# Holding back the q, k loads of later batches, and moving an interleave to the end of DVE's work, in a fused attention and MLP kernel

## The chip, the cores and the metric

The kernel runs on one core of a Trainium2 chip. The metric is device time in microseconds (us), the median of several executions; a profile is one execution, recorded by the hardware. Its "span" is a little shorter than the time (356.0 us against 357.73 us for the profiled execution of the kernel before).

Engines: PE multiplies matrices, ACT (ScalarE) does exp and gelu, DVE (VectorE) does copies, masks and reductions, POOL (GpSimd) is here mostly an issuer of DMAs, and SP (SyncE) is only an issuer of DMAs. Both issuers feed the same 16 DMA engines, through two queues: q0 is POOL's, q1 is SP's. (From 66 to 78 us of the profile before, the packets of q0 and q1 take 92.0% and 27.7% of the time of the 16 engines, over 100% together.)

## The reference

Attention with a causal mask and a cumulative decay over 8 batches, 8 heads, 576 positions and 64 channels, whose output, seen as 4608 tokens of 512 channels, goes through a two-layer MLP with an exact gelu.

```python
def _attn_ref(q, k, v, s):                      # (8, 8, 576, 64), s (8, 8, 576)
    scores = scale * np.matmul(q, k.transpose(0, 1, 3, 2))
    cum = np.cumsum(np.maximum(s, 0.0), axis=-1)
    bias = -(cum[:, :, :, None] - cum[:, :, None, :])
    scores = np.where(causal, -1000000000.0, scores + np.minimum(bias, 0.0))
    ...                                         # softmax over the last axis
    return np.matmul(attn, v)

def _moe_ref(x, w_in, w_out):                   # x (4608, 512), 512 -> 2048 -> 512
    h = x @ w_in
    g = 0.5 * h * (1.0 + erf(h * inv_sqrt2))
    return g @ w_out
```

## The kernel before

The MLP works through 9 chunks of 512 tokens, counted from 0. Chunk c does its own two layers and, between the matmuls of its second layer, the attention of batch c + 1 in four head pairs. So each chunk has the same work on PE, up to chunk 6.

Each batch's q and k take this path:

1. POOL loads them from HBM, cast to bf16, into one of **three** buffers (`bufs=3`), four loads to a batch. POOL issues them in program order, each as soon as its buffer is free: batch b + 3 follows when batch b has been consumed.
2. DVE interleaves the two heads of each pair (`interleave`).
3. SP writes the rows to a scratch in HBM (`write_rows`).
4. SP reads them back with DMA transposes into `qkT` (`transpose_rows`). Only then can PE compute scores.

Besides the interleave, DVE scales v, masks the exponentials of the scores before PE multiplies them with v, and takes maxima of q, k and v for a check of their range (`absmax`, `absmax_v`); `cert_decay` is one more such check, of the decay.

v goes another way: SP loads it, in five loads to a batch, with rows of 256 bytes. SP issues everything in program order, so the rows of a batch wait on SP behind the v loads of that batch (batch 2's rows, interleaved by 66.1 us, were issued at 81.75, after v loads whose issue ended at 80.27).

```python
def load_early(b, n, p, both=False):
    src = q if n == "q" else k
    if p == 0:
        early[b, n] = work.tile([128, 2, 2, G * D], bf16, tag=f"raw{n}", bufs=3, name=f"early_{n}")
    e0 = (p // 2) * 64
    out = early[b, n][e0 : e0 + 64, p % 2]
    if both:
        out = early[b, n][e0 : e0 + 64].rearrange("g j e f -> g (j e) f")
    ap = [[G * D, 64], [S * D, 4 if both else 2], [1, G * D]]
    nc.gpsimd.dma_start(out=out, in_=bass.AP(tensor=src.tensor, offset=..., ap=ap))

def load_qk(b):
    for p in (0, 2):
        for n in "qk":
            load_early(b, n, p, both=True)
...
# before the chunks
nc.gpsimd.tensor_copy(pace[:64], raws[1, "v"][:64, ST - 1, 0, 0:1])
load_qk(2)
load_qk(3)

for c in range(NCH):
    nb = c + 1
    ...                                          # first-layer matmuls, part 1
    if 0 < c and nb < B:
        if nb + 1 < B:
            load_v(nb + 1, [nc.sync])
        scale_v(nb, STS, nc.vector)
        if nb + 1 < B:
            for i, n in enumerate("qk"):
                interleave(nb + 1, n)
                write_rows(nb + 1, i, nc.sync)
            if nb + 2 < B:
                load_qk(nb + 2)
        absmax_v(nb)
    if c == 0:
        absmax_v(0)
    if c < B:
        for p in range(NP):
            absmax(c, p)
    for f2 in range(3, FT // 2):
        l1_item(c, f2)
    if c == 0:
        ...                                      # attention of batch 1; load_v(2); interleave(2),
        absmax_v(1)                              # write_rows(2), transpose_rows(2, p)
        cert_decay()
    elif nb < B:
        exp_set()
        l2_item(c, 0, 0, 4)
        sc_item(nb, 0)                           # scores of pair 0: needs qkT of batch nb
        l2_item(c, 0, 4)
        for p in range(1, NP):
            if nb + 1 < B:
                transpose_rows(nb + 1, p - 1)
            sc_item(nb, p)
            av_item(nb, p - 1)
            ...
```

The `pace` copy is a device that this kernel used already: a 128x1 copy on POOL that reads a tile. POOL works in order, so every load behind it waits until that tile has been written (the profile before has the copy at 51.58 us, after 21.33 us of waiting for v of batch 1, and batch 2's first load at 52.03). (`qkT`, as well as the v tile of a batch, has two buffers.)

Of the kernel before, what the change touches and what calls it, by code (L numbers as in the profile page):

```python
# [19 lines left out]
def kernel(  # L20
# [10 lines left out]
    nc = tc.nc  # L31
# [7 lines left out]
    B, H, S, D = q.shape  # L39
# [4 lines left out]
    NP = H // 2  # L44
# [51 lines left out]
# [9 lines that stand above are left out]
        nc.gpsimd.dma_start(  # L105
            out=out,
            in_=bass.AP(tensor=src.tensor, offset=src.offset + (b * H + 2 * p) * S * D, ap=ap),
        )
# [24 lines left out]
    qkT = [const.tile([128, 2, NP, 640], bf16, name=f"qkT{i}") for i in range(2)]  # L133
# [11 lines left out]
# [4 lines that stand above are left out]
# [3 lines left out]
    def interleave(b, n):  # L152
        i = 0 if n == "q" else 1
        t = qk_of[b, i] = work.tile([128, 2, G, 2, D], bf16, tag="qkbf", bufs=2, name="qk_bf")
        for j in range(2):
            nc.vector.tensor_copy(  # L156
                t[:, j].rearrange("g r e d -> g e r d"),
                early[b, n][:, j].rearrange("g e (r d) -> g e r d", r=G),
            )
# [3 lines left out]
    def write_rows(b, i, eng):  # L163
        rows_of[b, i] = t = dram.tile([2, 2, S, 128], bf16, name=f"rows{b}_{i}")
        eng.dma_start(
            out=t.rearrange("j a (g r) c -> (a g) j (r c)", r=G),
            in_=qk_of.pop((b, i)).rearrange("p j r e d -> p j (r e d)"),
        )
# [8 lines left out]
    def load_v(b, engs):  # L177
        if (b, "v") not in raws:
            v_tile(b)
        t = raws[b, "v"]  # L180
        for st in range(ST):
            n_st = 128 if st < ST - 1 else SL
            engs[st % len(engs)].dma_start(  # L183
                out=t[:n_st, st, :, :],
                in_=bass.AP(
                    tensor=v.tensor,
                    offset=v.offset + b * H * S * D + st * 128 * D,
                    ap=[[D, n_st], [S * D, H], [1, D]],
                ),
            )  # L190

    def absmax(b, p):

        nc.vector.tensor_reduce(  # L194
            amx[:, b * NP + p], qkT[b % 2][:, :, p, :S], axis=AX, op=ALU.max, apply_absolute_value=True
        )
# [238 lines left out]
    def av_rest(b, p):  # L435
        if p == 0:
            rest_of[b] = ps.tile([128, 2, NP, SL], fp32, tag="av", bufs=3, name="avr")
        for den in range(2):
            av_mm(b, p, rest_of[b][:, den, p], [(jt, 0, n, off) for jt, n, off in REST], den)

    def norm_rest(b):
        t = rest_of[b].rearrange("d n p i -> d n (p i)")
        norm(b, 0, NP, t[:, 0], t[:, 1], CUT, S, [(2, 0, NP * SL)])


    gT_of = {}
# [3 lines left out]
    def l1_item(c, f2, k0=0, k1=None, av=False):  # L450
        k1 = KO if k1 is None else k1
        if c not in gT_of:
            gT_of[c] = work.tile([128, FT, NB], bf16, tag="gT", bufs=1, name="gT")
        if k0 == 0 and av:
            h_of[c, f2] = [ps.tile([128, NB], fp32, tag="av", bufs=3, name="h1_ps") for _ in range(2)]
        elif k0 == 0:
            h_ps = ps.tile([128, 2, NB], fp32, tag="sc", bufs=2, name="h_ps")
            h_of[c, f2] = [h_ps[:, 0], h_ps[:, 1]]
            hh_of[c, f2] = h_ps
        for i in range(2):  # L460
            ft = f2 * 2 + i
            for ko in range(k0, k1):
                nc.tensor.matmul(  # L463
                    h_of[c, f2][i], lhsT=w_in_r[:, ko, ft * 128 : (ft + 1) * 128],
                    rhs=xT[:, ko, c * NB % XW : c * NB % XW + NB],
                    start=(ko == 0), stop=(ko == KO - 1),
                )
        if k1 == KO and f2 < FT // 2 - 1 and not av:
            nc.scalar.activation(gT_of[c][:, f2 * 2 : f2 * 2 + 2, :], hh_of[c, f2], func=AF.Gelu)  # L469
        elif k1 == KO:  # L470
            for i in range(2):
                nc.scalar.activation(gT_of[c][:, f2 * 2 + i, :], h_of[c, f2][i], func=AF.Gelu)  # L472
# [20 lines left out]
    def exp_set():  # L493
        nc.scalar.preload_act_table_set("natural_log_exp_and_others")
# [4 lines left out]
    pace = const.tile([128, 1], fp32, name="pace")  # L499

    def tr_pair(b, p):
        tr_item(b, p, 0)
        tr_item(b, p, 1)
# [47 lines left out]
    for c in range(NCH):  # L551
        nb = c + 1
        l1_item(c, 0, 0, KO - 1)
        l1_item(c, 1, 0, KO - 1)
        if c == 0:
            for p in range(NP):
                av_rest(0, p)
            norm_rest(0)
        l1_item(c, 0, KO - 1)
        l1_item(c, 1, KO - 1)  # L560
        l1_item(c, 2, av=True)
        if 0 < c and nb < B:
            if nb + 1 < B:
                load_v(nb + 1, [nc.sync])
            scale_v(nb, STS, nc.vector)
            if nb + 1 < B:
                for i, n in enumerate("qk"):
                    interleave(nb + 1, n)
                    write_rows(nb + 1, i, nc.sync)
                if nb + 2 < B:  # L570
                    load_qk(nb + 2)
            absmax_v(nb)
        if c == 0:
            absmax_v(0)
        if c < B:
            for p in range(NP):
                absmax(c, p)
        for f2 in range(3, FT // 2):
            l1_item(c, f2)
        if c == 0:  # L580
            exp_set()
            l2_item(c, 0, av=True)
            tr_pair(1, 0)
            tr_pair(1, 1)
            l2_item(c, 1, 0, 4)
            tr_pair(1, 2)
            l2_item(c, 1, 4, 8)
            tr_pair(1, 3)
            sc_item(1, 0)
            l2_item(c, 1, 8)  # L590
            load_v(2, [nc.sync])
            sc_item(1, 1)
            l2_item(c, 2, 0, 6, av=True)
            sc_item(1, 2)
            scale_pair(1, 0)
            l2_item(c, 2, 6, 12, av=True)
            sc_item(1, 3)
            l2_item(c, 2, 12, av=True)
            scale_pair(1, 1)
            l2_item(c, 3, 0, 4)  # L600
            interleave(2, "q")
            write_rows(2, 0, nc.sync)
            av_item(1, 0, rest=False)
            scale_pair(1, 2)
            scale_pair(1, 3)
            l2_item(c, 3, 4, 8)
            interleave(2, "k")
            write_rows(2, 1, nc.sync)
            av_item(1, 1, wide=True, rest=False)
            l2_item(c, 3, 8, 12)  # L610
            for p in (0, 1):
                transpose_rows(2, p)
            av_rest(1, 0)
            av_rest(1, 1)
            av_item(1, 2, wide=True)
            l2_item(c, 3, 12)
            av_item(1, 3)
            norm_rest(1)
            for p in (2, 3):
                transpose_rows(2, p)  # L620
            absmax_v(1)
# [4 lines that stand above are left out]
            sc_item(nb, 0)  # L626
# [6 lines that stand above are left out]
                l2_item(c, p, 0, 12)  # L633
                if p == NP - 1:
                    if nb + 1 < B:
                        transpose_rows(nb + 1, p)
                    av_item(nb, p)
                    norm_rest(nb)
                l2_item(c, p, 12)
        else:  # L640
            if c == B - 1:
                cert_1()
            for sub in range(4):
                l2_item(c, sub, av=sub % 2 == 0)
                if c == B - 1 and sub < 3:
                    (cert_2, cert_3, cert_4)[sub]()
# [151 lines left out]
```

## Time and profile before

| | before |
|---|---|
| time, median of 3 | 357.71 us (356.89 to 358.71) |
| span of the profiled execution | 356.0 us |
| PE busy | 322.6 us |
| mean granted clock of PE (1 is full speed) over the run | 0.972 |

The page of the profile: the span in 40 slices of 8.9 us; each digit is tenths of busy share, or tenths of full clock for PEclk.

```profile
PE   2788999992369999999999999999999999999993
...
PEclk9999999998569999999999999999999999999998
DMA  8999989999999599679346915773440110011011
```

Between its start and its end PE is busy nearly all the time, except in slices 9 to 11 (counted from 0), some 80 to 106 us, where its clock falls too. The DMA engines are at 80% or more nearly all the time up to there. The stage table puts a number on it; its windows run from the first first-layer matmul of one chunk to that of the next, for chunks 1, 2 and 3, and its columns are the length of the window, busy time of each engine with the number of instructions, granted clock, DMA share and GB/s.

```profile
67.44:121.19 53.75, 38.90 (x271) 19.13 (x265) 27.60 (x59) 25.47 (x38) 4.28 (x7) 0.84 1.07 207
121.19:155.75 34.56, 34.56 (x266) 17.66 (x265) 22.25 (x41) 23.95 (x35) 2.45 (x4) 1.00 0.87 188
155.75:190.30 34.55, 34.55 (x265) 17.64 (x264) 22.24 (x40) 23.94 (x35) 0.00 (x0) 1.00 0.61 134
```

Chunk 1 takes 53.75 us for work that takes chunks 2 and 3 34.56 and 34.55 us: 19.2 us are lost there. PE's timeline (start, duration, and in brackets the idle time before it with its releaser):

```profile
94.36 1.03 PE L357 MATMUL sc_ps<-qkT 64*128 64x256 bf16 x10 [12.07 <-DMA qkT<-rows]
95.33 5.14 PE L482 MATMUL o_ps<-w_out_r,gT 128*128 128x512 bf16 x12
103.26 0.76 PE L357 MATMUL sc_ps<-qkT 64*128 64x256 bf16 x10 [2.79 <-DMA qkT<-rows]
```

PE waits 12.07 us for batch 2's first transposes and 2.79 us for the second pair's. Twelve second-layer matmuls right after the long wait take 5.14 us, at a granted clock of 0.53; in other chunks they take 2.76.

The chain of waits, followed back from PE, in order of time (start, duration, what):

```profile
55.49 0.48 SPq L183
...
58.34 7.79 SPq L183
...
66.17 6.86 SPq L183
...
73.07 7.20 SPq L183
...
82.23 7.45 DMA rows<-qk_bf
...
92.21 11.00 DMA qkT<-rows
```

Line 183 is the issue of a v load. SP is stuck in the five v loads of batch 2 from 55.49 to 80.27 us, so it issues the rows of batch 2 at 81.75, although DVE had finished the interleave at 66.1. What POOL issues at that time (its timeline; the first line belongs to batch 4, the second to batch 5, the third to batch 6):

```profile
56.85 0.71 POOL L105 DMA_DIRECT2D early_q<-in_q_dram  x1
...
65.26 1.02 POOL L105 DMA_DIRECT2D early_q<-in_q_dram  x1 [1.45 <-DVE vv L211]
...
89.50 0.61 POOL L105 DMA_DIRECT2D early_q<-in_q_dram  x1 [18.33 <-DVE qk_bf L156]
```

And the DMA queues between 66 and 78 us (packets, MB, share of the time of 16 engines):

```profile
q0 software_dynamic: 1765, 1.91, 92.0%
q1 hardware_dynamic: 1764, 0.44, 27.7%
```

Both queues move the same number of packets, 1765 and 1764, while q0 moves over four times the bytes. (In each stretch of 2 us from 62 to 82 us the two counts differ by at most 2, for instance 295 and 293 from 66 to 68.) From 12 us and 16 engines, one pair takes 12,000 x 16 / 1765 = 109 ns. A 256 KB v load is 1024 rows of 256 bytes. Spread evenly that is 64 to an engine, and 64 x 109 ns = 7.0 us: an estimate, and close to what an issue takes there (6.86 to 7.79 us).

### The profile page before, as it was taken

What the parts mean: (1) busy time and instruction counts of PE and PEld (TensorE: products, weight loads), DVE (VectorE), ACT (ScalarE), POOL (GpSimd) and SP (SyncE); (2) the same over time, 40 slices, a digit from 0 to 9 for tenths busy, and PEclk for the clock granted to TensorE, in tenths of its full rate; (3) what the DMA queues carried; (4) which work ended last, traced back from release to release, by engine and by line L of the source; (5) the groups of instructions that cost most, each with busy time, mean ns of one, the idle gap of its engine ahead of it and who ended that gap; (6) DMA issues with size and microseconds to landing.
All of it is one profiled execution on the core that took longest, in us unless ns stands there. A gap on an engine that the chain in (4) does not pass through costs nothing.

```text
span 356.0 us, 6297 instructions
## 1 busy us (share of the span) xinstructions
PE 322.6 (91%) x2538; PEld 164.6 (46%) x2538; DVE 197.8 (56%) x387; ACT 202.1 (57%) x286; POOL 39.1 (11%) x63
## 2 busy tenths in 40 slices
PE   2788999992369999999999999999999999999993
PEld 1554454640135545544554445445544554444441
DVE  5596476952934595469446934784476448050021
ACT  2776618773233768576867577667676757403500
POOL 6593016300200020000000000000000000000000
PEclk9999999998569999999999999999999999999998
DMA  8999989999999599679346915773440110011011
GB/s 161 156 202 174 197 167 186 199 198 275 126 193 289 149 181 271 137 136 256 46 115 134 225 49 125 150 196 64 125 65 0 47 45 31 0 62 58 1 61 65
DMA packets 88244, 47.30 MB, mean 133 GB/s; under 512 B 68176, under 2 KB 80464, under 8 KB 88208
## 3 DMA queue, kind: packets, MB, share of 16 engines
q1 hardware_dynamic: 75216, 33.19, 40.2%
q0 software_dynamic: 12992, 13.63, 24.0%
q8 instruction: 22, 0.36, 0.4%
q14 instruction: 14, 0.11, 0.1%
HBM read 36.85 MB, written 16.52 MB: 150 GB/s over the span
## 4 chain that ended last, share of the span: by engine, by line
PE 70%; DMA 14%; SPq 9%; POOL 4%; ACT 1%; DVE 1%; issue 0%; ACTq 0%
PE o_ps L482 31%; PE h_ps L463 27%; SPq L183 7%; DMA early_k<-in_k_dram 6%; PE sc_ps L357 4%; PE avn L385 4%; DMA raw_v<-in_v_dram 3%; DMA qkT<-rows 3%; PE avd L385 3%; DMA rows<-qk_bf 2%; POOL P L377 1%; PE avr L385 1%; POOL w_in_r L228 1%; POOL w_out_r L228 1%; POOL P L372 1%; SPq L172 1%
## 5 line engine op out<-in xcount | busy, mean ns | idle before, releaser
L482 PE MATMUL o_ps<-w_out_r,gT 128*128 128x512 bf16 x576 | 136.0, 386 | 0.0
L463 PE MATMUL h_ps<-xT,w_in_r 128*128 128x512 bf16 x576 | 126.3, 379 | 1.3 <-DVE xT L418 0.7
L363 ACT ACTIVATE P<-sc_ps 128x1024 bf16<-128x1024 f32 x64 | 62.0, 1021 | 60.6 <-PE sc_ps L357 60.5
L463 PEld LDWEIGHTS <-w_in_r 128*128 128x128 bf16 x576 | 56.1, 98 | 69.1 <-issue 1.9
L482 PEld LDWEIGHTS <-gT 128*128 128x128 bf16 x576 | 53.6, 99 | 62.9 <-issue 3.8
L469 ACT ACTIVATE gT<-h_ps 128x1024 bf16<-128x1024 f32 x54 | 54.3, 1023 | 47.1 <-PE h_ps L463 47.0
L489 DVE COPY o_sb<-o_ps 128x512 f32<-128x512 f32 x36 | 24.8, 688 | 59.1 <-PE o_ps L482 59.1
L372 DVE TENSOR_TENSOR P<-P,tri_bf 128x512 bf16<-128x512 bf16 x61 | 25.7, 424 | 44.3 <-ACT P L363 43.6
L194 DVE TENSOR_REDUCE amx<-qkT 128x2 f32<-128x1152 bf16 x32 | 40.9, 1333 | 0.0
L357 PE MATMUL sc_ps<-qkT 64*128 64x256 bf16 (+2 forms) x320 | 22.9, 270 | 18.5 <-DMA qkT<-rows 14.9
L418 DVE SCALAR_TENSOR_TENSOR xT<-avn,ln 128x256 bf16<-128x256 f32 (+3 forms) x64 | 21.6, 385 | 26.2 <-ACT ln L403 26.2
L211 DVE TENSOR_TENSOR vv<-raw_v,wb 128x512 bf16<-128x512 f32 (+2 forms) x46 | 27.2, 645 | 9.1 <-DMA raw_v<-in_v_dram 9.1
L357 PEld LDWEIGHTS <-qkT 64*128 64x128 bf16 x320 | 14.2, 100 | 33.7 <-DMA qkT<-rows 16.1
L402 ACT ACTIVATE ln<-avd 128x256 f32<-128x256 f32 x56 | 18.6, 390 | 12.1 <-PE avd L385 12.0
L403 ACT ACTIVATE ln<-ln 128x512 f32<-128x512 f32 (+1 forms) x40 | 23.5, 587 | 1.3
L472 ACT ACTIVATE gT<-h_ps 128x512 bf16<-128x512 f32 x36 | 19.6, 602 | 6.3 <-PE h_ps L463 6.3
L201 DVE TENSOR_REDUCE amv<-raw_v 128x1 f32<-128x2048 f32 (+1 forms) x16 | 22.9, 1468 | 0.0
L385 PEld LDWEIGHTS <-vv 128*64 128x64 bf16 x384 | 17.7, 115 | 8.5 <-issue 4.0
L105 POOL DMA_DIRECT2D early_q<-in_q_dram x18 | 12.0, 664 | 58.2 <-DVE qk_bf L156 52.9
L385 PEld LDWEIGHTS <-wb 128*64 128x64 bf16 x384 | 18.1, 117 | 0.4
L385 PE MATMUL avn<-P,vv 128*64 128x256 bf16 x224 | 17.0, 276 | 0.2 <-DVE vv L211 0.2
L385 PE MATMUL avd<-P,wb 128*64 128x256 bf16 x224 | 16.2, 269 | 0.0
(81 smaller groups left out, 140.1 us busy)
## 6 DMA issues: line engine op xcount, KB each, us to landing
out_dram<-o_sb SPq DMA_DIRECT2D x36, 256.0 KB, 2.2
raw_v<-in_v_dram SPq DMA_DIRECT2D x32, 256.0 KB, 5.3
rows<-qk_bf SPq DMA_DIRECT2D x12, 576.0 KB, 5.0
early_q<-in_q_dram POOLq DMA_DIRECT2D x14, 288.0 KB, 11.5
early_k<-in_k_dram POOLq DMA_DIRECT2D x14, 288.0 KB, 12.7
w_in_r<-in_moe_w_in_dram POOLq DMA_DIRECT2D x4, 512.0 KB, 8.2
w_out_r<-in_moe_w_out_dram POOLq DMA_DIRECT2D x4, 512.0 KB, 10.9
raw_v<-in_v_dram SPq DMA_DIRECT2D x8, 128.0 KB, 5.2
```

The costliest lines, as they stand in the source:

```text
L183: engs[st % len(engs)].dma_start(out=t[:n_st, st, :, :], in_=bass.AP(tensor=v.tensor, offset=v.offset + b * H * S * D + st * 128 * D, ap=[ ...
L194: nc.vector.tensor_reduce(amx[:, b * NP + p], qkT[b % 2][:, :, p, :S], axis=AX, op=ALU.max, apply_absolute_value=True)
L211: eng.tensor_tensor(vb[:n_st, st0:st1, h0:h1, :], t[:n_st, st0:st1, h0:h1, :], wb[:n_st, st0:st1, b * H + h0 : b * H + h1] .unsqueeze(3).t ...
L357: nc.tensor.matmul(s_ps[:, e, off : off + n], lhsT=qkT[b % 2][e * 64 : e * 64 + 64, 1, p, jt * 128 : jt * 128 + 128], rhs=qkT[b % 2][e * 6 ...
L363: nc.scalar.activation(P[:, :, UO[u] : UO[u] + UW[u]], s_ps[:, :, : UW[u]], func=AF.Exp, scale=scale)
L372: eng.tensor_tensor(d, d, tri_bf.unsqueeze(1).unsqueeze(1).to_broadcast([128, 2, 2, 128]), op=MULT)
L385: nc.tensor.matmul(out[e * 64 : e * 64 + 64, lo : lo + n], lhsT=(wb[:, jt, b * H + h : b * H + h + 1].to_broadcast([128, 64]) if den else ...
L403: nc.scalar.activation(ln[:, :w], ln[:, :w], func=AF.Exp, scale=-1.0)
L463: nc.tensor.matmul(h_of[c, f2][i], lhsT=w_in_r[:, ko, ft * 128 : (ft + 1) * 128], rhs=xT[:, ko, c * NB % XW : c * NB % XW + NB], start=(ko ...
L469: nc.scalar.activation(gT_of[c][:, f2 * 2 : f2 * 2 + 2, :], hh_of[c, f2], func=AF.Gelu)
L482: nc.tensor.matmul(o_ps, lhsT=gT[:, ft, sub * 128 : (sub + 1) * 128], rhs=w_out_r[:, ft, :], start=(ft == 0), stop=(ft == FT - 1),)
L489: nc.vector.tensor_copy(o_sb, o_ps)
```

## The change

Its intent: keep batches 4 to 7 out of POOL's queue while SP's v loads, rows and transposes need the DMA engines. Batch 4 waits for the last transposed k of batch 2; batches 5 to 7 wait for the first gelu of chunks 2 to 4. Besides, the interleave moves behind the absmax groups, last of DVE's work in layer 1.

```diff
             scale_v(nb, STS, nc.vector)
-            if nb + 1 < B:
-                for i, n in enumerate("qk"):
-                    interleave(nb + 1, n)
-                    write_rows(nb + 1, i, nc.sync)
-                if nb + 2 < B:
-                    load_qk(nb + 2)
             absmax_v(nb)
         if c == 0:
             absmax_v(0)
         if c < B:
             for p in range(NP):
                 absmax(c, p)
+        if 0 < c and nb + 1 < B:
+            for i, n in enumerate("qk"):
+                interleave(nb + 1, n)
+                write_rows(nb + 1, i, nc.sync)
+            if nb + 2 < B:
+                nc.gpsimd.tensor_copy(
+                    pace, qkT[nb % 2][:, 1, NP - 1, 0:1] if c == 1 else gT_of[c][:, 0, 0:1]
+                )
+                load_qk(nb + 2)
```

## The prediction

> **What bounds the kernel now.** Mostly PE: the page shows it busy 322.6 of 356.0 us. By the stage table, chunks 2 and 3 (counted from 0, first-layer start to the next) take 34.56 and 34.55 us, PE busy throughout; chunk 1, the same work, takes 53.75 (67.44 to 121.19). These 19.2 us are the only large loss. PE's timeline shows them: idle 12.07 us before the scores of batch 2, pair 0 (94.36) and 2.79 us before pair 1 (103.26), both waiting for batch 2's transposes, and matmuls at half clock around them (12 second-layer matmuls in 5.14 us, otherwise 2.76). [...] granted clock over chunk 1 is 0.84, later 1.00.

> **Why the transposes are late.** In the chain of waits SP issues the five v loads of batch 2 from 55.5 to 80.3 us (all five take 4.85 us in chunk 3). So the rows write of batch 2 starts at 81.75, though its interleaves ended at 66.1, and lands near 88.3. Meanwhile POOL issued q, k of batches 2 to 5 (52.0 to 71.2). In the DMA records POOL's queue and SP's alternate packet by packet, about 100 ns for a q/k packet (1,152 B), 30 ns for a v packet (256 B)[...]. A 256 KB v load then takes 6.9 us, as seen; a batch of q, k 7.4 us of all engines.

> **What the change does.** It adds only four 128x1 POOL copies (about 0.2 us each; POOL is idle). Batches 4 and 5 no longer enter the queue at 57 and 65: batch 4 waits for the last transpose of batch 2, batches 5 to 7 for the first gelu of chunks 2 to 4. Interleave moves behind the absmax groups, 8 us later on DVE (2.86 + 5.11); masks find DVE as before. In later chunks this is hidden: SP reaches the rows write at that time or has over 20 us left.

> **Estimate, from those packet rates.** POOL's queue runs dry near 69 instead of 84; the v issues end near 71.5, rows are issued at 72.5 and land near 77.5; pair 0's transposes land near 81 to 82, pair 1's near 85. PE wants pair 0 at 82.3, pair 1 at 86. So the stall falls from 14.9 us to 0 to 3, the clock stays up, chunk 1 takes 34.6 to 38 us. Then batch 4 (from about 91) competes with v of batch 3; its rows land near 104, transposes from 104 to 115, wanted from 117: room, but only some us. Batches 5 to 7 get over 20 us before their interleave.

> **Prediction:** 357.7 - 19.2 + about 0.8 = 339.3 us, range 337.3 to 345.5. Faster by over 2%: 0.95; within 2%: 0.04; slower: 0.01.

> **What would show it right:** issue of batch 2's v loads shrinks from 24.8 to about 16 us; rows issued at 71 to 74; PE's wait for transposes below 3 us; granted clock near 1.00 through chunk 1, which takes 34.5 to 38 us; chunks 2 to 8 and everything before 56 us unchanged; PE busy about 5 us less.

> **What would make it wrong:** q/k of batches 2 and 3 alone keep SP back beyond 75 us[...]; or batch 4's load, now against v of batch 3, or the later interleave, delays batch 3's transposes beyond 117 us and the stall returns in chunk 2; or batch 4 is late for its interleave.

Three passages that did not rest on this case's traces are cut at the marks. No term of the sum is among them: it came to 357.7 - 19.2 + about 0.8 = 339.3 us, as it stands. That the clock stays up with a stall of 0 to 3 us was the estimate; no run had shown it, and in the kernel before the clock was at 0.50 right after a wait of 2.79 us. The packet times are those of the profile before from 66 to 78 us: 92.0% of 12 us x 16 engines over 1765 packets is 100 ns, 27.7% over 1764 is 30 ns. The 7.4 us for a batch of q, k are an estimate, its 1.18 MB at the 1.91 MB that q0 moved in those 12 us.

## The result

| | before | after |
|---|---|---|
| time, median | 357.3 us (4 runs, the three above and one more, 355.85 to 358.71) | 340.75 us (4 runs, 340.72 to 342.19) |
| span of the profiled execution | 356.0 us | 338.9 us |
| PE busy | 322.6 us | 318.1 us |
| mean granted clock | 0.972 | 0.995 |

The ratio is 0.9547, with a 95% interval of 0.95 to 0.9594. Ratios here are the mean time of one kernel's fast runs over that of the other's of the same rounds, so not quite the ratio of the medians quoted. A run counts as slow when it is over 1.5% above the fastest of the same kernel.

The page after, the lines of PE and of its clock:

```profile
PE   1778999999899999999999999999999999999993
...
PEclk9999999999999999999999999999999999999997
```

The hole in PE and in its clock is gone. The stage table after, chunks 1, 2 and 3:

```profile
66.99:102.84 35.85, 34.76 (x270) 17.78 (x265) 26.78 (x59) 25.47 (x38) 2.65 (x5) 1.00 0.86 204
102.84:137.40 34.56, 34.56 (x266) 17.66 (x265) 22.34 (x41) 23.95 (x35) 2.86 (x5) 1.00 0.98 206
137.40:172.40 35.00, 34.71 (x265) 17.62 (x264) 22.23 (x40) 23.94 (x35) 2.65 (x5) 1.00 0.91 182
```

Chunk 1 went from 53.75 to 35.85 us. Chunk 3, however, went from 34.55 to 35.00. PE's timeline in chunk 1 after:

```profile
81.78 0.77 PE L357 MATMUL sc_ps<-qkT 64*128 64x256 bf16 x10
82.48 2.76 PE L482 MATMUL o_ps<-w_out_r,gT 128*128 128x512 bf16 x12
...
86.90 0.69 PE L385 MATMUL avn<-P,vv 128*64 128x256 bf16 x8 [1.09 <-DVE P L372]
```

No wait for transposes at all; the only one left, 1.09 us, is for masks from DVE. In SP's timeline the five v loads, the two rows writes and the first four transposes of batch 2:

```profile
55.05 15.12 SPq L183 DMA_DIRECT2D raw_v<-in_v_dram  x5
...
70.93 0.99 SPq L165 DMA_DIRECT2D rows<-qk_bf  x2
76.61 5.16 SPq L172 DMA_TRANSPOSE qkT<-rows  x4
```

The v loads' issue shrank from 24.77 to 15.12 us, and the first transposes are issued at 76.61 instead of 88.31. POOL's timeline shows the copies and what they held back: batch 4 until 89.71, batch 5 until 108.09.

```profile
89.20 0.18 POOL L577 CAST pace<-qkT 128x1 f32<-128x1 bf16 x1 [33.19 <-DMA qkT<-rows]
89.71 0.62 POOL L105 DMA_DIRECT2D early_q<-in_q_dram  x1 [0.33 <-issue]
...
107.58 0.39 POOL L577 CAST pace<-gT 128x1 f32<-128x1 bf16 x1 [15.40 <-ACT gT L469]
108.09 0.62 POOL L105 DMA_DIRECT2D early_q<-in_q_dram  x1
```

The sum of the spans: 17.90 us gained in chunk 1, 0.45 us because chunk 1 began earlier (66.99 against 67.44), and 1.35 us lost in chunks 3, 4 and 5, which took 35.00, 35.01 and 35.01 us instead of 34.55, 34.56 and 34.56. That makes 17.0 of the 17.1 us between the spans.

Two things were left to explain: which part of the change does the work, and where the 1.35 us in chunks 3 to 5 come from. In ACT's timeline, the beginning of chunk 3's gelus before:

```profile
156.48 0.42 ACT L403 ACTIVATE ln<-ln 128x256 f32<-128x256 f32 x1
156.92 1.28 ACT L469 ACT_TABLE_LOAD   x1
158.97 1.94 ACT L469 ACTIVATE gT<-h_ps 128x1024 bf16<-128x1024 f32 x2 [0.77 <-PE h_ps L463]
```

and after:

```profile
140.66 1.28 ACT L469 ACT_TABLE_LOAD   x1 [2.11 <-PE h_ps L463]
141.96 1.94 ACT L469 ACTIVATE gT<-h_ps 128x1024 bf16<-128x1024 f32 x2
```

Before, ACT loads the gelu table while PE is still computing, and then waits 0.77 us. After, ACT waits 2.11 us for PE first and loads the table then, so 1.28 us of load stand between the matmul and the gelu (the chunk gets 0.45 us longer by it). The compiled program and the trace have the reason: POOL's copy reads the gelu tile, that tile has one buffer, so the next chunk's first gelu must wait for POOL; the gelu instruction carries that wait, and the wait for the matmul has become an instruction of its own in front of the table load (at L469 the trace after has four such wait instructions of ACT, the first at 140.6 us, just before the load; the trace before has one, at 325.5 us). In short (this is a summary and no view of the profile):

```
before:  L469 LoadActFuncSet
         L469 Activation gT<-h_ps 128x1024 [waits PE] x2
after:   wait for PE
         L469 LoadActFuncSet
         L469 Activation gT<-h_ps 128x1024 [waits Pool]
         L469 Activation gT<-h_ps 128x1024 [waits PE]
```

### The profile page after: what moved, and what is told of

The parts are those of the page before. It is cut to its first block, busy times and chain, and to the rows that moved or that the text cites. A ratio compares the mean times of both kernels' runs of the same rounds, so it can differ in the third digit from the quotient of the medians.

```text
span 338.9 us, 6313 instructions
## 1 busy us (share of the span) xinstructions
PE 318.1 (94%) x2538; PEld 163.0 (48%) x2538; DVE 197.7 (58%) x387; ACT 202.1 (60%) x286; POOL 35.5 (10%) x67
## 4 chain that ended last, share of the span: by engine, by line
PE 83%; DVE 8%; ACT 5%; DMA 2%; issue 1%; POOL 0%; ACTq 0%; DVEq 0%; POOLq 0%
PE o_ps L482 37%; PE h_ps L463 30%; PE sc_ps L357 5%; PE avn L385 4%; PE avd L385 3%; DVE qkT L345 2%; DMA early_k<-in_k_dram 2%; ACT L469 2%; DVE amx L194 1%; PE avw L385 1%; DVE amv L201 1%; DVE vv L211 1%; ACT gT L469 1%; PE avr L385 1%; PE tr_ps L340 1%
## 5 line engine op out<-in xcount | busy, mean ns | idle before, releaser
L482 PE MATMUL o_ps<-w_out_r,gT 128*128 128x512 bf16 x576 | 133.0, 380 | 0.0
L469 ACT ACTIVATE gT<-h_ps 128x1024 bf16<-128x1024 f32 x54 | 54.3, 1023 | 42.2 <-PE h_ps L463 41.8
L489 DVE COPY o_sb<-o_ps 128x512 f32<-128x512 f32 x36 | 24.8, 688 | 58.3 <-PE o_ps L482 57.3
L372 DVE TENSOR_TENSOR P<-P,tri_bf 128x512 bf16<-128x512 bf16 x61 | 26.5, 437 | 40.5 <-ACT P L363 39.9
```

The lines of the kernel that those rows point to most:

```text
L372: eng.tensor_tensor(d, d, tri_bf.unsqueeze(1).unsqueeze(1).to_broadcast([128, 2, 2, 128]), op=MULT)
L469: nc.scalar.activation(gT_of[c][:, f2 * 2 : f2 * 2 + 2, :], hh_of[c, f2], func=AF.Gelu)
L482: nc.tensor.matmul(o_ps, lhsT=gT[:, ft, sub * 128 : (sub + 1) * 128], rhs=w_out_r[:, ft, :], start=(ft == 0), stop=(ft == FT - 1),)
L489: nc.vector.tensor_copy(o_sb, o_ps)
```

## The experiments

The theory: the gain comes from taking batches 4 and 5 out of POOL's queue, because POOL's and SP's queues alternate packet by packet (1765 and 1764 packets in 12 us) and SP cannot get its v loads out. Rivals: that the order on DVE carries the gain, and that the DMA engines share bytes rather than packets.

The table has one row for each kernel that ran: the median, and the length of chunks 1, 2, 3 and 4 in the profiled execution, read off PE's timeline from one first-layer start to the next.

| kernel | time, us | chunk 1 | chunk 2 | chunk 3 | chunk 4 |
|---|---|---|---|---|---|
| before | 357.3 | 53.75 | 34.56 | 34.55 | 34.56 |
| the change | 340.75 | 35.85 | 34.56 | 35.00 | 35.01 |
| e1 holding only | 341.0 | 35.84 | 34.55 | 35.01 | 35.01 |
| e2 order only | 349.96 | 45.81 | 34.55 | 34.56 | 34.55 |
| e3 batch 4 not held | 345.28 | 39.66 | 34.56 | 35.00 | 35.01 |
| e4 only batch 4 held | 348.17 | 35.84 | 44.49 | 34.55 | 34.56 |
| g3 the same again | 343.94 (one fast run) | 35.85 | 37.45 | 34.55 | 34.56 |
| g1 before, batch 6 held | 350.78 | 46.27 | 34.55 | 34.56 | 34.55 |
| f4 before, half-length q, k packets | 355.58 | 46.88 | 34.55 | 34.56 | 34.56 |
| g2 the same from batch 2 on | 354.74 | 49.94 | 34.56 | 34.55 | 34.56 |
| f1 change, waits on absmax | 339.94 | 35.84 | 34.55 | 34.56 | 34.56 |
| f2 change, checks later | 339.82 | 34.56 | 35.86 | 35.01 | 35.01 |
| f3 both | 338.26 | 34.57 | 34.55 | 34.56 | 34.56 |

All kernels gave correct results. The kernel before measured 356.52 (e runs), 357.39 (f runs) and 357.62 us (g runs) on the same chips.

### e1: holding back only

```diff
 (from the change; the interleave goes back to its old place)
             scale_v(nb, STS, nc.vector)
+            if nb + 1 < B:
+                for i, n in enumerate("qk"):
+                    interleave(nb + 1, n)
+                    write_rows(nb + 1, i, nc.sync)
             absmax_v(nb)
 ...
         if 0 < c and nb + 1 < B:
-            for i, n in enumerate("qk"):
-                interleave(nb + 1, n)
-                write_rows(nb + 1, i, nc.sync)
             if nb + 2 < B:
```

> Only the holding back; the interleave stays at its old place ahead of the absmax groups. Theory (the held loads alone free SP's v loads of batch 2): within 0.3% of the full change, 340 to 342 us, v issues of batch 2 in about 15 us, no wait for transposes in chunk 1, and the 1.1 us wait for masks in chunk 1 still there, since DVE has the same sum of work ahead of them. Rival (the order on DVE carries the gain or part of it): 345 us or more.

Measured: 341.0 us (340.62 to 341.08), v issues in 14.03 us, no wait for transposes in chunk 1, and the same wait of 1.09 us for masks. The stage table, chunk 1:

```profile
66.89:102.73 35.84, 34.75 (x269) 17.76 (x266) 26.76 (x59) 25.46 (x38) 3.39 (x5) 1.00 0.95 211
```

The holding alone gives the whole gain, and the masks' wait does not come from the interleave's new place.

### e2: the order only

```diff
 (from the change)
             if nb + 2 < B:
-                nc.gpsimd.tensor_copy(
-                    pace, qkT[nb % 2][:, 1, NP - 1, 0:1] if c == 1 else gT_of[c][:, 0, 0:1]
-                )
                 load_qk(nb + 2)
```

> Only the interleave moved behind the absmax groups; no load held back. Theory: batches 4 and 5 still queue against v of batch 2, so SP's v issues still take about 25 us and pair 0's scores still wait about 12 us; but batch 6, released by the interleave of batch 3, now starts some 5 us later, so the transposes of pair 1 meet less traffic and the second wait of 2.8 us may go: 352 to 358 us. Rival (the order carries the gain): below 348 us.

Measured: 349.96 us; fast runs 349.68 to 349.98 and one slow run, 355.41; ratio 0.9807 (0.9735 to 0.9879: faster, but not clearly by 2%). This is more than expected: about 40% of the gain of the whole change, from a part that e1 showed to be unnecessary. In SP's timeline the v loads' issue still takes 24.32 us, so the first collision is untouched. PE's timeline:

```profile
91.45 1.03 PE L357 MATMUL sc_ps<-qkT 64*128 64x256 bf16 x10 [9.52 <-DMA qkT<-rows]
...
96.09 0.61 PE L357 MATMUL sc_ps<-qkT 64*128 64x256 bf16 x10
```

The first wait fell from 12.07 to 9.52 us and the one before pair 1 is gone. POOL starts batch 6 at 94.88 instead of 89.50, because it waits for the interleave of batch 3, which has moved back. So there might be a second collision in the kernel before, of batch 6 with the transposes of batch 2, or else DVE's order itself helps. g1 was made to tell these apart.

### e3: batch 4 not held

```diff
             if nb + 2 < B:
-                nc.gpsimd.tensor_copy(
-                    pace, qkT[nb % 2][:, 1, NP - 1, 0:1] if c == 1 else gT_of[c][:, 0, 0:1]
-                )
+                if c > 1:
+                    nc.gpsimd.tensor_copy(pace, gT_of[c][:, 0, 0:1])
                 load_qk(nb + 2)
```

> The change, but batch 4 is not held (batches 5 to 7 are). Three batches of q, k stand against v of batch 2, where before had four and the change has two. Theory of shared packets: POOL's queue is dry about 7 us later than in the change, v issues take about 22 us, rows go out near 78 to 79, pair 0's transposes land near 88, PE waits 5 to 8 us and then runs some 3 us at half clock: 346 to 351 us. Rival (only an overload by batch 5, whose load waits for the interleave, matters): 340 to 342 us.

Measured: 345.28 us (343.53 to 345.74). The v issues took 21.65 us and the rows went out at 77.60, both as expected; the rows landed within 4 us, faster than in the kernel before, so PE waited 3.58 us instead of the expected 5 to 8, and the time came out just below its range. PE's timeline:

```profile
85.56 1.04 PE L357 MATMUL sc_ps<-qkT 64*128 64x256 bf16 x10 [3.58 <-DMA qkT<-rows]
86.53 3.96 PE L482 MATMUL o_ps<-w_out_r,gT 128*128 128x512 bf16 x12
```

So the dose counts: with two, three and four batches in POOL's queue, the v issues take 15.1, 21.7 and 24.8 us. After the wait of 3.58 us the matmuls were slow too (3.96 us for twelve instead of 2.76). So they were after a shorter wait: in the kernel before, the granted clock was 1.00 again during the wait of 2.79 us that ended at 103.26 (from 101 to 103 us), and 0.50 right after it:

```profile
104.00:107.00 3.00, 3.00 (x29) 1.94 (x28) 0.99 (x3) 2.91 (x5) 0.00 (x0) 0.50 0.96 203
```

In e4's profile, which is a slow one, twelve matmuls took 4.45 us after a wait of 2.25 us; in g3's, a fast one, the granted clock was 1.00 from 103 to 139 us, with waits of 1.84 and 0.78 us. How long a wait has to be for half clock, and whether the single wait decides it, was not shown.

### g1: the kernel before, with batch 6 held

```diff
 (from the kernel before)
                 if nb + 2 < B:
+                    if c == 3:
+                        nc.gpsimd.tensor_copy(pace, amx[:, 2 * NP + NP - 1, 0:1])
                     load_qk(nb + 2)
```

> The kernel before with one POOL copy more: batch 6 (and with it 7) waits for the last absmax of chunk 2; batches 4 and 5 and the order on DVE stay as before. In the order-only run the second wait was nearly gone. Theory (its gain came from batch 6, which the old order releases at 88 to 89 us, into the transposes of batch 2): the v issues still take 24 to 25 us, pair 0 waits 9 to 10 us, the second wait of 2.8 us is gone, 349 to 351 us, like the order alone. Rival (the gain came from DVE, whose absmax group no longer stands ahead of the masks): no gain here, 355 to 358 us.

Measured: 350.78 us (349.62 to 352.07), ratio 0.981 (0.9744 to 0.9877). SP's v issues took 24.18 us. PE's timeline has one wait for transposes, and no second one:

```profile
91.00 1.03 PE L357 MATMUL sc_ps<-qkT 64*128 64x256 bf16 x10 [9.11 <-DMA qkT<-rows]
```

DVE's order is the old one here, and the gain is that of e2. So the order's gain was the later start of batch 6: shown. In the kernel before there are two collisions, batches 4 and 5 with the v loads of batch 2, and batch 6 with its transposes. The change removes both by its copies, since batch 6 is behind them in POOL's order; with the loads held, the order has nothing left to give.

### e4 and g3: only batch 4 held

```diff
             if nb + 2 < B:
-                nc.gpsimd.tensor_copy(
-                    pace, qkT[nb % 2][:, 1, NP - 1, 0:1] if c == 1 else gT_of[c][:, 0, 0:1]
-                )
+                if c == 1:
+                    nc.gpsimd.tensor_copy(pace, qkT[nb % 2][:, 1, NP - 1, 0:1])
                 load_qk(nb + 2)
```

> The change, but only batch 4 is held by a copy; batches 5 to 7 follow as soon as their buffers are free and nothing reads gT on POOL. Theory: chunk 1 as in the change (35.9 us); batch 5 now queues right behind batch 4 against v and transposes of batch 3, which has some 10 us of slack, so no new wait in chunk 2; and chunks 3 to 5 lose the 0.45 us each that the change added (the gelu table load waits for the matmul there), so 339 to 340 us, 1 to 1.4 us below the change. Rival (holding 5 to 7 is needed): a wait for transposes in chunk 2 and 343 us or more.

Measured: 348.17 us; fast runs 344.06, 347.37 and 348.98, and the profiled one, 349.58, marked slow. This expectation failed: I had overlooked that batch 6's buffer is free by then too, so three batches follow the copy and not two. As the profile was slow, the same kernel ran again:

> The same kernel as the run in which only batch 4 is held, for a profile that is not marked slow. Theory: the wait has moved into chunk 2, where batches 4, 5 and 6 now follow one another from 89 us on: transposes of batch 3 first issued near 110 us, PE waits for them and for the masks behind DVE, 344 to 349 us. Rival (the waits seen there belong to the slow state): 339 to 341 us.

Measured: 343.94 us in the profiled run, which is fast, and 349.20 in one marked slow. The waits are in the fast profile too. PE's timeline in chunk 2:

```profile
121.20 0.61 PE L357 MATMUL sc_ps<-qkT 64*128 64x256 bf16 x10 [1.84 <-DMA qkT<-rows]
125.29 0.61 PE L357 MATMUL sc_ps<-qkT 64*128 64x256 bf16 x10 [0.78 <-DMA qkT<-rows]
```

POOL issued batches 4, 5 and 6 one behind the other from 92.12 to 107.13 us, and SP issued batch 3's first transposes at 108.02, against 103.21 in the change. The collision has moved one chunk on. So something has to hold back the loads behind batch 4 too; whether each of the copies for batches 5 to 7 is needed was not tested. (Why this kernel's own times spread over 5 us is not settled; in chunk 2 of the slow profile, after its wait of 2.25 us, twelve second-layer matmuls took 4.45 us and, after one of 3.17 us, sixteen took 5.65; in the fast one twelve took 2.76.) Chunks 3 to 5 take 34.55 us here, where nothing on POOL reads the gelu tile.

### f4 and g2: packets of half the length

These test the packet theory in the kernel before, with nothing held back. The same bytes of q and k arrive in twice as many packets.

```diff
 (from the kernel before; f4 has "if both:", g2 "if both and b > 1:"; some lines joined)
         ap = [[G * D, 64], [S * D, 4 if both else 2], [1, G * D]]
+        if both and b > 1:
+            for a0 in (0, G * D // 2):
+                nc.gpsimd.dma_start(
+                    out=out[:, :, a0 : a0 + G * D // 2],
+                    in_=bass.AP(tensor=src.tensor, offset=src.offset + (b * H + 2 * p) * S * D + a0,
+                                ap=[[G * D, 64], [S * D, 4], [1, G * D // 2]]),
+                )
+            return
```

> The kernel before, nothing held back, but each q, k load of batches 1 to 7 issued as two of half the row length, so that its packets are 576 B written instead of 1,152: same bytes, twice the packets. Theory (POOL's and SP's queues alternate packet by packet, so v of batch 2 pays one q/k packet for each of its own): a q/k packet costs some 50 to 65 ns instead of 100, a 256 KB v load is issued in 4 to 5 us instead of 6.9, the five in about 17 us, and the stall before chunk 1's scores shrinks by some 5 us or more: 347 to 353 us. Rival (v gets a share of the bytes, whatever the packets): v issues stay at 24 us or more, no faster than before.

Measured: 355.58 us; fast runs 351.99 to 355.77, one slow, 357.56; ratio 0.9912, so the same within 2%. The five v issues took 15.29 us, as the packet theory has it, but the time was outside its range: the split slowed batch 1's loads as well, and chunk 1 began at 72.13 us instead of 67.44. g2 leaves batch 1 alone.

> The half-length q, k loads again, but only for batches 2 to 7, as the first trial also slowed batch 1's loads and with them chunk 0 (chunk 1 began at 72.1 instead of 67.4). Theory (packet by packet): chunk 1 begins at 67 to 68 again, the five v issues take 15 to 18 us, the rows write still meets q, k packets and lands 9 to 12 us after its issue, pair 0 waits 5 to 8 us: 349 to 353 us. Rival (a share of bytes): v issues 24 us or more, 356 us or more.

Measured: 354.74 us (353.23 to 355.68), ratio 0.9919, the same within 2% and above the expected range; chunk 1 began at 66.94. The queues between 62 and 72 us, and SP's timeline:

```profile
q0 software_dynamic: 2311, 1.26, 87.9%
q1 hardware_dynamic: 2312, 0.58, 43.7%
```

```profile
54.98 15.60 SPq L193 DMA_DIRECT2D raw_v<-in_v_dram  x5
...
72.89 1.41 SPq L175 DMA_DIRECT2D rows<-qk_bf  x2
84.91 6.22 SPq L182 DMA_TRANSPOSE qkT<-rows  x4
```

Again the packet counts are equal, and a pair now takes 10,000 x 16 / 2311 = 69 ns instead of 109. With the bytes of q and k unchanged, the v loads' issue shrank from 24.8 to 15.6 us. The rival, a share of bytes, is refuted: what SP got here is one packet for each packet of POOL's (2312 for 2311).

The second half of the expectation failed: PE's first wait was 13.47 us, not 5 to 8. The rows' packets alternated with q and k as well (from 63 to 85 us, the rows among it, the counts are 4532 and 4526), and they landed 12 us after their issue, and the first transposes went out at 84.91, only 3.4 us earlier than before; batch 6 started at 86.11, right among them. Speeding up the v loads did not help here, as the rows met the same traffic; holding the traffic back helped both (the change's rows were issued at 70.93, its first transposes at 76.61, and PE waited for none).

### f1: waiting on absmax instead of gelu

```diff
-                    pace, qkT[nb % 2][:, 1, NP - 1, 0:1] if c == 1 else gT_of[c][:, 0, 0:1]
+                    pace, qkT[nb % 2][:, 1, NP - 1, 0:1] if c == 1 else amx[:, c * NP + NP - 1, 0:1]
```

> The change, but batches 5 to 7 wait for DVE's last absmax of the chunk instead of the chunk's first gelu, so that POOL never reads the gelu tile. Theory (that read makes the next chunk's first gelu wait for POOL, and pushes its wait for the matmul in front of the table load, whose 1.28 us then stand open): the table load of chunks 3 to 5 runs early again, chunks 3 to 5 go from 35.0 back to 34.55 us, total 339.2 to 339.8. Rival (the 0.45 us per chunk comes from the loads' place in time, not from the read): no change, 340.7 to 341.

Measured: 339.94 us (339.41 to 340.92). Chunks 3 to 5 took 34.56 us each, and the table load runs early again:

```profile
138.68 1.28 ACT L469 ACT_TABLE_LOAD   x1
140.73 1.94 ACT L469 ACTIVATE gT<-h_ps 128x1024 bf16<-128x1024 f32 x2 [0.77 <-PE h_ps L463]
```

In the median this is 0.8 us below the change, and as the two were timed in different rounds the difference alone would be weak. Chunks 3, 4 and 5 take 35.0 us in all four kernels where POOL reads the gelu tile (the change, e1, e3, f2) and 34.55 or 34.56 in all nine profiles where it does not, whenever their loads are issued (batch 5's from 94.54 in g3, from 118.50 in f1, against 108.09 in the change).

### f2: the decay checks later

```diff
             absmax_v(1)
-            cert_decay()
 ...
                 l2_item(c, p, 12)
+            if c == 4:
+                cert_decay()
```

> The change, but the decay checks (1.9 us of small DVE work ahead of chunk 1's scaling of v) are done at the end of chunk 4. Theory (DVE's sum of work, not any load, holds chunk 1's first masks, and so PE, for the last 1.1 us): PE's wait for masks in chunk 1 goes from 1.1 us to under 0.3, total 339.5 to 340. Rival (the v loads of batch 2 hold DVE): the scaling then waits for v, and the 1.1 us stay.

Measured: 339.82 us (339.18 to 340.90). Chunk 1 takes 34.56 us, so the wait for masks was DVE's sum of work: 1.9 us of small checks stood at the front of a chain of scaling, absmax and interleave. In the profiled run chunk 2 had a wait for pair 1's transposes of batch 3, so the saving was given back there; at 340.90 us it is the slowest of the six runs, so the others need not have had that wait:

```profile
121.09 0.61 PE L357 MATMUL sc_ps<-qkT 64*128 64x256 bf16 x10 [1.24 <-DMA qkT<-rows]
```

This wait is not in the profiles of the change, e1, f1 and f3. The slack there is thin: in the change, batch 5's load starts at 108.09, among the transposes of batch 3 (issued from 103.21 to 119.80).

### f3: both

> Both of the above on top of the change: each saving is in another chunk, so they should add: 338.0 to 338.9 us, every chunk from 1 to 7 within 0.3 us of 34.55.

Measured: 338.26 us (337.78 to 338.36), ratio 0.948 to the kernel before. It beats both kernels. The stage table, chunk 1:

```profile
66.88:101.45 34.57, 34.20 (x265) 17.63 (x265) 25.24 (x46) 24.79 (x37) 2.65 (x5) 1.00 0.91 198
```

Every chunk from 1 to 6 is now within 0.02 us of 34.55. Chunk 7, which the expectation counted in, has no attention left to do and takes 28.28 us. (PE's busy time in this table is slightly low, as some matmul records are missing: 265 here, 270 in the change's chunk 1.) What is left is the start, the work of chunk 0, and PE's own work.

## Why the prediction was right or wrong

- **The size: right.** 339.3 us were predicted and 340.75 measured, inside 337.3 to 345.5. The 19.2 us of chunk 1 were the right ceiling: 17.90 of them came back. That the total came so close is in part luck: chunk 1 kept 1.3 us instead of the 0.8 allowed for, chunks 3 to 5 lost 1.35 that were not forecast, and an earlier start of chunk 1, not forecast either, gave 0.45 back.
- **The mechanism of the v loads: right.** The two queues alternated packet by packet (1765 to 1764 before, 2311 to 2312 in g2, where a pair of half-length packets took 69 ns instead of 109 and the v issues 15.6 us). Issue of the v loads: about 16 us predicted, 15.1 measured. Rows issued at 71 to 74: 70.9. First transposes issued after the rows landed near 77.5: 76.6. Clock 1.00 through chunk 1: so it was. PE busy about 5 us less: 4.5.
- **The cause of the whole stall: incomplete.** "Batches 4 and 5 no longer enter the queue at 57 and 65" was given as the reason for all of the stall. The runs show a second collision: holding batch 6 alone (g1), or just delaying it by the order on DVE (e2), takes 7.5 to 7.9 us off chunk 1. I had seen batch 6 start at 89.5, among the transposes, and had not counted it. The total was right nevertheless, and to that extent by luck, because the change removes both and the parts overlap: 7.9 us from the order alone, 17.9 from holding alone, 17.9 from both.
- **"Masks find DVE as before": true, but the wrong conclusion was drawn.** With the interleave in its old place the masks wait just as long (e1), so its move did not delay them; the error was to take DVE's unchanged work as free. The 0.8 us that I kept back for a remaining stall were meant for transposes, whose wait became 0. What remained was 1.09 us for masks, out of 1.3 us by which chunk 1 exceeds the others, and it came from DVE's sum of work (f2). Before, that sum was hidden behind the long stall: PE's waits there include none for masks.
- **"Chunks 2 to 8 ... unchanged": wrong for chunks 3 to 5.** I costed the copies as 0.2 us each on an idle engine (measured: 0.18 us, one 0.39). Their cost is not on POOL: by reading the gelu tile they put a new wait on ACT, which moved the table load into the path, 0.45 us in each of three chunks (gone in f1 and f3).
- **The risk that was named: right in kind.** Batch 3's first transposes were issued at 103.2, predicted 104, and nothing was waited for in chunk 2. But the slack is thin: f2's profile shows it used up, with a wait of 1.24 us, and with batches 5 and 6 in the queue behind batch 4 (e4, g3) the stall returns in chunk 2.
